# A memory-bound add in 64 KiB rows: wider loads of x and a wider middle store in the same queue

## The chip, the cores and the metric

One core of one Trainium2 chip. The metric is the device time of one execution in microseconds, lower is better. A value quoted for a kernel is the median of its runs.

## The reference, cut to what matters

```python
B, S, D = 512, 32, 640                  # x, fx: bfloat16
def reference(x, fx, alpha):            # alpha: one bfloat16
    return x + alpha * fx
```

Each of x, fx and the output holds 20.97 MB. Reading two and writing one moves 62.92 MB, and nothing can be left out.

## The kernel before

The tensors are seen as 128 partitions of 81,920 elements (160 KiB) each. A *unit* here is 16,384 elements of each partition: a row of 32 KiB on each partition, 4 MiB in all. Five units make a tensor. All large transfers are issued from SyncE (SP), and so go through one first-in-first-out queue. The add works in place in x's buffer, on VectorE (DVE).

```python
CHUNK = 16384
xs = ctx.enter_context(tc.tile_pool(name="xs", bufs=4))   # 4 x 32 KiB a partition
fs = ctx.enter_context(tc.tile_pool(name="fs", bufs=2))   # 2 x 32 KiB
...
    def compute(k, parts=1):
        n = CHUNK // parts
        for j in range(parts):
            s = bass.ts(j, n)
            nc.vector.scalar_tensor_tensor(
                out=xt[k][:, s], in0=ft[k][:, s], scalar=a_f[:],
                in1=xt[k][:, s], op0=ALU.mult, op1=ALU.add)
...
    load_x(0); load_f(0); load_x(1); load_f(1); load_x(2)      # one line each in the source
    compute(0); load_f(2); store(0); load_x(3)
    compute(1); load_f(3); store(1); load_x(4)
    compute(2); load_f(4); store(2)
    compute(3); store(3)
    compute(4, 2); store(4, 0, 2); store(4, 1, 2)              # last unit in two halves
```

In the queue this reads, with x0 for the load of unit 0 of x, f0 for that of fx, and S0 for the store of unit 0:

```
x0 f0 x1 f1 x2 f2 S0 x3 f3 S1 x4 f4 S2 S3 S4a S4b
```

Of the kernel before, what the change touches and what calls it, by code (L numbers as in the profile page):

```python
# [1 line left out]

# [4 lines left out]

ACT = mybir.ActivationFunctionType
ALU = mybir.AluOpType
F32 = mybir.dt.float32  # L10
BF16 = mybir.dt.bfloat16

CHUNK = 16384


def alpha_to_lanes(nc, consts, psum, alpha, eng):

    P = nc.NUM_PARTITIONS
    a_1 = consts.tile([1, 1], alpha.dtype, name="a_1")
    eng.dma_start(out=a_1[:], in_=alpha[None, :])  # L20
    ones = consts.tile([1, P], alpha.dtype, name="ones")
    nc.vector.memset(ones[:], 1.0)  # L22
    a_ps = psum.tile([P, 1], F32, name="a_ps")
    nc.tensor.matmul(a_ps[:], ones[:], a_1[:], start=True, stop=True)  # L24
    a_f = consts.tile([P, 1], F32, name="a_f")
    nc.vector.tensor_copy(out=a_f[:], in_=a_ps[:])  # L26
    return a_f


@with_exitstack  # L30
def kernel(
    ctx: ExitStack,
    tc: tile.TileContext,
    x: bass.AP,
    fx: bass.AP,
    alpha: bass.AP,
    out: bass.AP,
):
    nc = tc.nc
    P = nc.NUM_PARTITIONS  # L40
    xv = x.flatten_outer_dims().rearrange("(p n) d -> p (n d)", p=P)
    fxv = fx.flatten_outer_dims().rearrange("(p n) d -> p (n d)", p=P)
    ov = out.flatten_outer_dims().rearrange("(p n) d -> p (n d)", p=P)
    F = xv.shape[1]
    K = F // CHUNK
    assert K * CHUNK == F and K == 5

    consts = ctx.enter_context(tc.tile_pool(name="consts", bufs=1))
    psum = ctx.enter_context(tc.tile_pool(name="psum", bufs=1, space=bass.MemoryType.PSUM))
    xs = ctx.enter_context(tc.tile_pool(name="xs", bufs=4))  # L50
    fs = ctx.enter_context(tc.tile_pool(name="fs", bufs=2))
    ctx.enter_context(tc.manual_schedule())

    a_f = alpha_to_lanes(nc, consts, psum, alpha, nc.scalar)
    xt, ft = {}, {}

    def load_x(k):
        xt[k] = xs.tile([P, CHUNK], x.dtype, tag="x", name="x_t")
        nc.sync.dma_start(out=xt[k][:], in_=xv[:, bass.ts(k, CHUNK)])  # L59

    def load_f(k):
        ft[k] = fs.tile([P, CHUNK], fx.dtype, tag="f", name="f_t")
        nc.sync.dma_start(out=ft[k][:], in_=fxv[:, bass.ts(k, CHUNK)])

    def compute(k, parts=1):
        n = CHUNK // parts
        for j in range(parts):
            s = bass.ts(j, n)
            nc.vector.scalar_tensor_tensor(  # L69
                out=xt[k][:, s],  # L70
                in0=ft[k][:, s],
                scalar=a_f[:],
                in1=xt[k][:, s],
                op0=ALU.mult,
                op1=ALU.add,
            )

    def store(k, j=0, parts=1):
        n = CHUNK // parts
        nc.sync.dma_start(  # L80
            out=ov[:, k * CHUNK + j * n : k * CHUNK + (j + 1) * n],
            in_=xt[k][:, bass.ts(j, n)],
        )

    load_x(0)
    load_f(0)
    load_x(1)
    load_f(1)
    load_x(2)
    compute(0)  # L90
    load_f(2)
    store(0)
    load_x(3)
    compute(1)
    load_f(3)
    store(1)
    load_x(4)
    compute(2)
    load_f(4)
    store(2)  # L100
    compute(3)
    store(3)
    compute(4, 2)
    store(4, 0, 2)
    store(4, 1, 2)


# [1 line left out]
_INS = ['x', 'fx', 'alpha']  # L109
_OUTS = [((512, 32, 640), 'bfloat16')]  # L110


# [23 lines left out]
```

## Time and profile before

| | |
|---|---|
| time, median of 3 runs | 152.81 us (152.61 to 152.85) |
| span of the profiled run | 150.6 us |
| moved | 62.92 MB, 418 GB/s over the span |
| queue's share of 16 DMA engines | 98.0% |
| DVE busy | 86.9 us, 58% |

The first lines are from the page of the kernel before: busy time by engine; then the span in 40 equal slices, where a digit is the busy share in tenths and GB/s is what was moved; then the queue with its packets, megabytes and share of 16 engines.

```profile
PE 0.2 (0%) x1; PEld 0.1 (0%) x1; DVE 86.9 (58%) x8; POOL 0.2 (0%) x4
...
DMA  6999999999999999799999999999999999999994
GB/s 200 444 453 435 418 418 418 418 444 453 444 453 435 418 418 418 339 444 470 418 418 418 418 418 435 435 435 453 426 435 444 418 418 435 435 435 405 426 444 205
DMA packets 2306, 62.92 MB, mean 418 GB/s; under 512 B 258, under 2 KB 258, under 8 KB 258
...
q1 hardware_dynamic: 2304, 62.92, 98.0%
```

DMA reads 9 everywhere but at the two ends and in the slice from 60 to 64 us, where the bytes moved fall to 339 GB/s. DVE is idle for 42% of the time. So the question is how many bytes the DMA engines move per microsecond, and nothing else. The page's chain of waits and its groups look different at first sight:

```profile
DMA 56%; DVE 29%; DVEq 6%; issue 0%; SPq 0%
...
L69 DVE SCALAR_TENSOR_TENSOR x_t<-f_t,a_f,x_t 128x16384 bf16<-128x16384 bf16 (+1 forms) x6 | 86.6, 14439 | 49.5 <-DMA f_t<-in_fx_dram 49.5
...
```

The chain says that DVE's last add was released by f_t loads, and the group says that DVE waited 49.5 us for them. Both are true, and neither is a cost: while DVE waits, the queue that it waits for is full. A wait is worth something only if the thing waited for could have started earlier.

The trace also records each packet of each DMA engine. Here a packet of data is one row of one transfer: 128 rows over 16 engines, 8 for each engine, back to back. The median packet took 1213 ns for a 32 KiB row (1792 packets) and 611 ns for a 16 KiB row (256 packets). Two halves take 9 ns more than a whole. Behind its rows, each DMA sends one more packet of 4 bytes on each engine, its *completion packet*; that the DMA has *landed* is told by a semaphore event some 0.4 us later.

### The profile page before, as it was taken

How to read it: one execution, taken by the hardware profiler on the slowest of the kernel's cores; microseconds unless marked ns; L12 is line 12 of the kernel's file. 1: busy time of each engine (PE TensorE's matmuls, PEld its weight loads, DVE VectorE, ACT ScalarE, POOL GpSimd, SP SyncE). 2: the span in 40 equal slices, each digit the busy share in tenths (PEclk: the TensorE clock that was granted, in tenths of full speed). 3: DMA queues.
4: the chain of work that ended last, by engine and by line, in shares of the span. 5: the costliest groups of instructions: out<-in, count | busy, mean ns of one | idle time of the engine just before them, and what ended most of it. 6: DMA issues, size and time to landing. Idle time of an engine off the chain costs nothing.

```text
span 150.6 us, 85 instructions
## 1 busy us (share of the span) xinstructions
PE 0.2 (0%) x1; PEld 0.1 (0%) x1; DVE 86.9 (58%) x8; POOL 0.2 (0%) x4
## 2 busy tenths in 40 slices
PE   0000000000000000000000000000000000000000
PEld 0000000000000000000000000000000000000000
DVE  0000009999679998499991006999900089997000
POOL 0000000000000000000000000000000000000000
DMA  6999999999999999799999999999999999999994
GB/s 200 444 453 435 418 418 418 418 444 453 444 453 435 418 418 418 339 444 470 418 418 418 418 418 435 435 435 453 426 435 444 418 418 435 435 435 405 426 444 205
DMA packets 2306, 62.92 MB, mean 418 GB/s; under 512 B 258, under 2 KB 258, under 8 KB 258
## 3 DMA queue, kind: packets, MB, share of 16 engines
q1 hardware_dynamic: 2304, 62.92, 98.0%
q10 hardware_dynamic: 2, 0.00, 0.0%
HBM read 41.94 MB, written 20.97 MB: 418 GB/s over the span
## 4 chain that ended last, share of the span: by engine, by line
DMA 56%; DVE 29%; DVEq 6%; issue 0%; SPq 0%
DMA f_t<-in_fx_dram 56%; DVE x_t L69 29%; DVEq L131 6%; SPq L59 0%; DVEq L69 0%
## 5 line engine op out<-in xcount | busy, mean ns | idle before, releaser
L69 DVE SCALAR_TENSOR_TENSOR x_t<-f_t,a_f,x_t 128x16384 bf16<-128x16384 bf16 (+1 forms) x6 | 86.6, 14439 | 49.5 <-DMA f_t<-in_fx_dram 49.5
L26 DVE COPY a_f<-a_ps 128x1 f32<-128x1 f32 x1 | 0.2, 159 | 1.1 <-PE a_ps L24 1.1
L22 DVE MEMSET ones<- 1x128 bf16 x1 | 0.2, 165 | 0.8 <-PEq L120 0.8
L24 PE MATMUL a_ps<-a,ones 1*128 1x1 bf16 x1 | 0.2, 159 | 1.9 <-DMA a<-in_alpha_dram 1.9
L120 POOL MEMSET const-bfloat16-1.0<- 128x1 bf16 x1 | 0.1, 102 | 0.0
L120 POOL MEMSET const-uint8-127<- 128x1 uint8 x1 | 0.1, 102 | 0.0
L24 PEld LDWEIGHTS <-ones 1*128 1x128 bf16 x1 | 0.1, 100 | 1.0 <-DVE ones L22 1.0
L120 POOL MEMSET const-float32-0.0<- 128x1 f32 x1 | 0.1, 99 | 0.2 <-issue 0.2
L120 POOL MEMSET const-float32-1.0<- 128x1 f32 x1 | 0.1, 99 | 0.0
## 6 DMA issues: line engine op xcount, KB each, us to landing
x_t<-in_x_dram SPq DMA_DIRECT2D x5, 4096.0 KB, 34.8
f_t<-in_fx_dram SPq DMA_DIRECT2D x5, 4096.0 KB, 32.1
out_dram<-x_t SPq DMA_DIRECT2D x4, 4096.0 KB, 36.5
out_dram<-x_t SPq DMA_DIRECT2D x2, 2048.0 KB, 15.2
a<-in_alpha_dram ACTq DMA_DIRECT2D x1, 0.0 KB
```

What stands on the lines that cost most here:

```text
L22: nc.vector.memset(ones[:], 1.0)
L24: nc.tensor.matmul(a_ps[:], ones[:], a_1[:], start=True, stop=True)
L26: nc.vector.tensor_copy(out=a_f[:], in_=a_ps[:])
L69: nc.vector.scalar_tensor_tensor(out=xt[k][:, s], in0=ft[k][:, s], scalar=a_f[:], in1=xt[k][:, s], op0=ALU.mult, op1=ALU.add,)
L120: nc = _bacc.Bacc("TRN2", target_bir_lowering=False, num_devices=1)
L131: with _tile.TileContext(nc) as tc:
```

## The change

It moves x in pairs of units, so that a row is 64 KiB long, stores units 1 and 2 together, and keeps everything that sets the start and the end (the first unit and the last two half stores) as it was. The intent is fewer and larger packets. The order of the queue changes with it: S0 now goes ahead of f2, and loads and stores alternate less often. (U is 16384, as CHUNK was.) Two slots of 64 KiB replace the four x slots; the first one holds x0 and f0 side by side at first.

```diff
-    xs = ctx.enter_context(tc.tile_pool(name="xs", bufs=4))
+    wide = ctx.enter_context(tc.tile_pool(name="wide", bufs=1))     # tags "a" and "b", 64 KiB each
     fs = ctx.enter_context(tc.tile_pool(name="fs", bufs=2))
...
+    t_0 = wide.tile([P, 2 * U], x.dtype, tag="a", name="t_0")
+    nc.sync.dma_start(out=t_0[:, :U], in_=xv[:, :U])
+    nc.sync.dma_start(out=t_0[:, U:], in_=fxv[:, :U])
+    def load_pair(tag, u):
+        t = wide.tile([P, 2 * U], x.dtype, tag=tag, name="x_t")
+        nc.sync.dma_start(out=t[:], in_=xv[:, u * U : (u + 2) * U])
+        return t
...
+    x_12 = load_pair("b", 1)
+    f_1 = load_f(1)
+    add(t_0[:, :U], t_0[:, U:])
+    store(0, t_0[:, :U])
+    f_2 = load_f(2)
+    add(x_12[:, :U], f_1[:])
+    x_34 = load_pair("a", 3)
+    f_3 = load_f(3)
+    add(x_12[:, U:], f_2[:])
+    f_4 = load_f(4)
+    store(U, x_12[:])
+    add(x_34[:, :U], f_3[:])
+    store(3 * U, x_34[:, :U])
+    ...                                # last unit: two half adds, two half stores, as before
```

The queue now reads, with wide transfers in brackets:

```
x0 f0 [x12] f1 S0 f2 [x34] f3 f4 [S12] S3 S4a S4b
```

## The prediction

> **What bounds the kernel now.** The DMA engines. In the page's forty slices DMA reads 9 in all but the first, the last and one slice near 60-64 us; the queue table says 98.0% of 16 engines' span for q1, and 62.92 MB at 418 GB/s. DVE is busy 58% and every wait of it (49.5 us) is for an f_t landing. The chain of waits names f_t loads for 56% and DVE for 29%, but that is only the order in which things were released: the one FIFO is never empty, so a DVE wait there costs nothing.
>
> From the packet records: one packet is one row on one engine, back to back. A 32 KiB row takes 1213 ns (median of 1792), a 16 KiB row 611 ns (256). So 16 KiB cost 602 ns (27.2 B/ns, 435 GB/s over 16 engines) plus about 9 ns fixed per packet. The Trainium skill, "DMA: Bandwidth & Descriptors", Specifications, gives 435 GB/s as the fabric ceiling; this trace agrees. Nothing in the change can beat that slope.
>
> Per engine: 112 x 1.213 + 16 x 0.611 = 145.6 us. The rest of the 150.6 us span: first packet at 1.74-2.15 us, its slow first row (+0.7 us), a stall of about 0.8 us at 57.5-61 us (the last fx rows before the first store), one of 0.2 us at 87.5-90 us (before the second store), a little engine skew, and 149.4 to 150.6 us for the last receipt and end.
>
> **What the change does.** Three transfers (two x pairs, the middle store) have 64 KiB rows. Estimate: 9 + 4 x 602 = 2417 ns against 2 x 1213 = 2426, so 24 packets per engine save 9 ns each: 0.2 us. All of it is on the critical path, since the DMA is. Packets in q1 fall by 384. The same section family of the skill ("Why small descriptors are slow") puts a fixed cost on a packet; at 32 KiB it is under 1%, as measured here.
>
> Order: x0 f0 x12 f1 | S0 f2 x34 f3 f4 S12 S3 S4a S4b. Switches from load to store fall from three to two, worth perhaps 0.1 us; I expect the 0.8 us stall of the first store to move to about 50 us and stay.
>
> **Does the FIFO run dry?** With 9.7 us per unit (the trace's landings): first five units end at 51.3; S0 is issued at 40.2. f2 follows at once. x34 needs slot a, S0 landed about 62, while f2 runs to 71: 9 us margin. f3 needs the first half-pair add, 51.5+17.3 = 69, needed at 90. f4 and S12 need the second, 72+17.3 = 89, needed at 100 (11 us margin). S3: add ends 118, needed 129. Last two halves: 127 and 136, needed 139 and 144. No gap. DVE work is unchanged: 87 us (17.28 us x4, 8.75 us x2). Head (32 KiB first unit) and tail (two 2 MiB stores) are the same as before.
>
> **Predicted:** 152.81 - 0.2 - 0.1 to 0.2: 152.5 us, range 151.9 to 153.2. Faster by 2% (below 149.8) 0.01: even free packets would save only 1.1 us. Within 2% 0.95. Slower 0.04.
>
> **What would show it.** Packets of 64 KiB in the records at about 2417 ns; q1 at 1920 packets; DMA slices 9 throughout but for one dip near 50 us; DVE busy 87 us; last store landing about 149.4 us.
>
> **What would make it wrong.** A 64 KiB row being cut into pieces by the descriptor generator (gain gone, count unchanged or higher); 64 KiB stores running slower than 27 B/ns; a landing of x12 or S0 late by over 9 us, seen as a DMA slice well below 9; a longer load-to-store stall.

## The result

The changed kernel took 152.66 us (median of 6 runs, 152.32 to 152.74), the kernel before in the same rounds 152.71 us (152.51 to 152.99). The ratio is 0.9992, with a 95% interval of 0.9977 to 1.0006: the same within 2%, and not told from no change at all. A ratio here is the mean time of one kernel's runs over that of the other's of the same rounds, so it is not quite the ratio of the medians quoted. Timed once more on another chip, below, the ratio was 0.9966 (0.9944 to 0.9988).

The same lines of the page of the changed kernel:

```profile
PE 0.2 (0%) x1; PEld 0.1 (0%) x1; DVE 86.8 (58%) x8; POOL 0.2 (0%) x4
...
DMA  6999996999999899999896969999996969898994
GB/s 226 417 452 426 426 556 278 556 434 400 400 426 426 278 417 417 434 478 512 382 538 295 556 278 426 478 434 426 434 565 295 556 278 556 365 426 373 447 434 178
DMA packets 1874, 62.92 MB, mean 417 GB/s; under 512 B 210, under 2 KB 210, under 8 KB 210
...
q1 hardware_dynamic: 1872, 62.92, 97.8%
```

The queue moved the same 62.92 MB in 1872 packets in place of 2304: 384 fewer rows (three wide transfers, 128 each), and 48 fewer completion packets, as three fewer DMAs each send 16. DVE is busy as before.

The DMA line looks worse now: 6, 8 and 9 change about, and GB/s goes from 278 to 556 and back. It is an artefact of the binning. A slice is 3.8 us and a 64 KiB packet lasts 2.4 us on all 16 engines nearly in step, so whole rows fall into one slice or the next: 16 rows of 64 KiB in 3.77 us are 278 GB/s, 32 are 556, and the two average 417. Spread over the slices that each packet covers, the packet records fill every slice but the first and the last. (They do so in the stall described below, too: packets there last longer, so a busy share cannot show it.) The run of the same order in 32 KiB rows, below, shows 9s there but for one slice. A reader who took the 6s for an idle queue would look for a wait that is not there.

The chain of waits of the changed kernel:

```profile
DVE 40%; DMA 35%; another core or an unknown queue 9%; DVEq 6%; SPq 0%; issue 0%
...
```

and the piece of it that is new, from the chain in order of time (start, duration, what):

```profile
22.88 17.28 DVE t L72
40.16 12.96 another core or an unknown queue
53.12 0.03 issue
...
```

There is one core, so no other core can have released this add. It is the load f1, issued at 2.11 us and landed at 53.1 us; presumably the view does not connect a landing with an issue 51 us old. It waited for nothing but its turn in the queue.

Whether the queue ran dry is read from the issue times (start, duration, engine and line) of SP:

```profile
...
40.19 0.35 SPq L77 DMA_DIRECT2D out_dram<-t  x1
40.58 0.44 SPq L68 DMA_DIRECT2D f_t<-in_fx_dram  x1
...
62.92 0.33 SPq L63 DMA_DIRECT2D x_t<-in_x_dram  x1
70.53 19.65 SPq L68 DMA_DIRECT2D f_t<-in_fx_dram  x2
...
90.24 46.39 SPq L77 DMA_DIRECT2D out_dram<-x_t  x4
...
```

S0 was issued at 40.19 us while f1 was still to come until 53 us. f2 followed it at 40.58. The pair x34 was issued at 62.92, when f2 kept the engines busy until 72; f3 at 70.53, needed at 91; f4 and S12 at 90, needed at 101 and 111. The tightest is S4b, the last store: it was issued at 136.3, and S4a landed at 144.6. The queue always had at least 8 us of work.

So the only terms left are packets and stalls. The completion events of each DMA say when it landed. The table has the mean of its 16 events, and gives the time from one landing to the next, in us. In the kernel before, each line is one unit:

| landed | before | order_only (new order, 32 KiB rows) | after |
|---|---|---|---|
| second transfer, f0 | 9.70 | 9.71 | 9.70 |
| x1, x2 or x12 | (x1) 9.72 | 9.72, 9.71 | 19.35 |
| last load ahead of S0 | (f2) 10.42 | (f1) 10.87 | (f1) 10.94 |
| S0 | 10.08 | 9.96 | 9.98 |
| load after S0 | (x3) 9.33 | (f2) 9.45 | (f2) 9.41 |
| x3, x4 or x34 | | 9.72, 9.71 | 19.35 |
| f3 | 9.88 | 9.72 | 9.72 |
| S1, then x4 (before only) | 9.86, 9.53 | | |
| f4 | 9.72 | 9.83 | 9.72 |
| S1 and S2, S2 alone, or S12 | (S2) 9.70 | 9.71, 9.67 | 19.33 |
| S3 | 9.66 | 9.68 | 9.67 |

(Left out of before: f1 9.71 and x2 9.72.) Undisturbed, a 32 KiB unit takes 9.715 us as a load and 9.66 us as a store. A pair in 64 KiB rows takes 19.352 us as a load, which is 0.078 us under two units, and 19.332 us as a store, which is 0.05 us under the two stores of order_only in the same place. That is 2 x 0.078 + 0.05 = 0.2 us, the amount that was predicted, but it flatters the change: the two stores of order_only stand behind a load and hold some of its second stall, and against two undisturbed stores (2 x 9.66) the wide one saves nothing.

Landings have a second fault. They come 0.3 to 0.5 us behind the completion packets, 0.5 to 0.9 us for a large store with a load behind it, and in most runs the lag grows while loads follow each other (0.36 to 0.47 us in before). From the completion packets of one DMA to those of the next (mean of 16), an undisturbed DMA takes 19.320 us in 64 KiB rows, 9.681 us in 32 KiB rows, 4.862 us for 2 MiB in 16 KiB rows and 2.453 us for 1 MiB in 8 KiB rows, loads and stores alike. So a wide transfer saves 2 x 9.681 - 19.320 = 0.042 us, and the three together 0.13 us. What is not constant is the stretch around S0, and that is what the experiments ask about.

In what follows, the *switch loss* of a run is the time from the landing ahead of that stretch to the landing behind it (last load ahead of S0, S0, next load), less 2 x 9.715 + 9.66 = 29.09 us. Before: 10.42 + 10.08 + 9.33 - 29.09 = 0.75 us. After: 10.94 + 9.98 + 9.41 - 29.09 = 1.24 us. The same sum over f3, S1 and x4 of before gives 0.17 us more for its second switch, while in the changed kernel f4 and S12 stand at the undisturbed values. By completion packets the losses at S0 read up to 0.2 us higher (0.90 us before, 1.33 after), and nearly all of it is in the load ahead of S0: f2 takes 10.57 us in before and f1 11.01 us in the changed kernel, in place of 9.68, while S0 and the load behind it are undisturbed in both. The 10.08 and 9.33 in the table are one late landing.

### The profile page after: what moved, and what is told of

Read it like the earlier page. It is cut to its first block, busy times and chain, and to the rows that moved or that the text cites. A ratio compares the mean times of both kernels' runs of the same rounds, so it can differ in the third digit from the quotient of the medians. Undisturbed runs are those within 1.5% of the kernel's fastest.

```text
span 150.9 us, 78 instructions
## 1 busy us (share of the span) xinstructions
PE 0.2 (0%) x1; PEld 0.1 (0%) x1; DVE 86.8 (58%) x8; POOL 0.2 (0%) x4
## 2 busy tenths in 40 slices
DMA packets 1874, 62.92 MB, mean 417 GB/s; under 512 B 210, under 2 KB 210, under 8 KB 210
## 3 DMA queue, kind: packets, MB, share of 16 engines
q1 hardware_dynamic: 1872, 62.92, 97.8%
## 4 chain that ended last, share of the span: by engine, by line
DVE 40%; DMA 35%; another core or an unknown queue 9%; DVEq 6%; SPq 0%; issue 0%
DVE x_t L72 29%; DMA f_t<-in_fx_dram 21%; DMA t<-in_fx_dram 14%; DVE t L72 11%; DVEq L121 6%; SPq L58 0%; DVEq L72 0%
## 5 line engine op out<-in xcount | busy, mean ns | idle before, releaser
L72 DVE SCALAR_TENSOR_TENSOR x_t<-f_t,a_f,x_t 128x16384 bf16<-128x16384 bf16 (+1 forms) x5 | 69.2, 13868 | 26.9 <-DMA f_t<-in_fx_dram 26.9
L72 DVE SCALAR_TENSOR_TENSOR t<-t,a_f 128x16384 bf16<-128x16384 bf16 x1 | 17.3, 17284 | 20.6 <-DMA t<-in_fx_dram 20.6
```

The lines of the kernel that those rows point to most:

```text
L72: nc.vector.scalar_tensor_tensor(out=x_ap, in0=f_ap, scalar=a_f[:], in1=x_ap, op0=ALU.mult, op1=ALU.add)
```

## The experiments

Twelve experiments were run, four of them repeats of a kernel, each on one chip with runs of the kernel before between. All gave the right result.

### Are the 64 KiB rows or the order behind the longer stall?

order_only keeps the new order and puts every row back to 32 KiB:

```diff
-        nc.sync.dma_start(out=t[:], in_=xv[:, u * U : (u + 2) * U])
+        for j in range(2):
+            nc.sync.dma_start(out=t[:, bass.ts(j, U)], in_=xv[:, (u + j) * U : (u + j + 1) * U])
...
-    store(U, x_12[:])
+    for j in range(2):
+        store((1 + j) * U, x_12[:, bass.ts(j, U)])
```

> The new order with every row back at 32 KiB (the pair loads and the middle store as two DMAs each). Theory A (64 KiB rows save only the fixed 8 ns of 24 packets per engine, and the longer stall before the first store belongs to the order or to chance): 152.85 us, 0.2 over the changed kernel, and the stall before the first store stays at 1.2 to 1.4 us per engine. Rival B (the wide rows ahead of it lengthen that stall from 0.95 to 1.3 us): stall back at 0.95 us, time 152.5 us.

Measured: 152.53 us (152.38 to 153.20, 6 runs) against 152.45 for before, ratio 1.0012 (0.9990 to 1.0033). Its profile is of the slowest of its runs, 153.20 us. The switch loss in it is 10.87 + 9.96 + 9.45 - 29.09 = 1.18 us.

```profile
DMA  6999999999999799999999999999999999999994
GB/s 216 433 450 424 416 416 433 433 450 450 442 424 416 277 416 467 433 433 433 441 424 416 424 459 442 424 442 433 398 416 424 433 467 433 433 433 394 424 429 173
```

The 6s and 8s of the changed kernel are gone, and one dip stays, 277 GB/s in the slice from 49 to 53 us. That is the stall, which in before stood near 60 us. So a stall of this length needs no wide rows, against rival B; it is one profile, and the changed kernel itself varies from 0.94 to 1.24 us (below). The time cannot tell 152.85 from 152.5 with this spread. By completion packets order_only also lost 0.25 us in f4, ahead of its second switch; all ten profiles with wide rows in this order lost under 0.06 us there. Whether the wide rows do that is not shown by one profile.

### What does a packet cost?

rows_8k is the kernel before with each transfer cut into DMAs of 8 KiB rows, four for one (two for each half store):

```diff
+    ROW = 4096
+    def cut(dst, src, n):
+        for i in range(n // ROW):
+            s = slice(i * ROW, (i + 1) * ROW)
+            nc.sync.dma_start(out=dst(s), in_=src(s))
```

> The kernel before with all rows cut to 8 KiB, four DMAs for one. Theory A (every packet has a fixed 8 to 9 ns): 8 KiB packets of about 310 ns, 4 x 310 - 1213 = 27 ns more per 32 KiB, 120 units of 32 KiB per engine: 3.2 us slower, 156 us. Rival (the fixed part is hidden when packets follow each other, and 1213 against 611 is rounding of the records): within 0.5 us of before.

Measured: 154.25 us against 152.45, ratio 1.0113 (1.0093 to 1.0132). Slower by 1.8 us, not by 3.2.

```profile
DMA  5999999999999999999999999999999999999995
GB/s 165 425 425 434 419 417 425 423 421 421 425 421 417 428 421 421 421 432 419 436 419 419 425 425 419 436 419 423 432 417 421 423 428 421 436 423 434 419 430 213
DMA packets 8642, 62.92 MB, mean 413 GB/s; under 512 B 962, under 2 KB 962, under 8 KB 962
...
q1 hardware_dynamic: 8640, 62.92, 98.8%
```

The medians of all data packets seen, where they were not disturbed (for 8 KiB, the stores), lie on one line, 8 ns + 301 ns for each 8 KiB:

| row | 512 B | 8 KiB | 16 KiB | 24 KiB | 32 KiB | 64 KiB |
|---|---|---|---|---|---|---|
| packet, ns | 27 | 309 | 611 | 912 | 1213 | 2418 |

But these 8 ns are not all time of the queue: neighbouring records overlap by 3 to 4 ns. By completion packets (2.453, 4.862, 9.681 and 19.320 us, above) a DMA costs 0.042 us beside its bytes, which is 4.7 ns for each of the nine packets that it sends on an engine. So a packet's fixed cost is real, but the rival was half right: some 4 of the 9 ns are hidden. For the 1.8 us this gives 1.8 us of packets, and two other things, which nearly cancel. The loads ran at 2.453 us for 1 MiB at first and, from about 15 us on, at 2.485 us, another 1.05 us in all. And this run had no switch loss: by landings, 4 MiB in 8 KiB rows took 9.94 us as loads and 9.73 as stores (0.225 and 0.07 us more than in 32 KiB rows), and the three transfers around S0 took 29.65 us, against 2 x 9.94 + 9.73 = 29.61. GB/s above has no dip anywhere. Before, by completion packets, all time above the undisturbed pace was 1.13 us, so 1.8 + 1.05 - 1.13 = 1.7 us is left, near the 1.8 measured.

That was the surprise: cutting all rows to a quarter removed the stall that the change was expected to keep. Whether it was removed, or paid in small parts by the slower loads (1.05 us against 1.13), is not shown. The next runs tried to buy this for less.

### Does the first store of the program pay?

The stall of before was large at its first store (0.75 us), small at its second (0.17) and none at its third. So a first store might pay for all. early_store adds a small first store, which the last store writes over:

```diff
+    E = 256
+    z = consts.tile([P, E], x.dtype, name="z")
+    nc.gpsimd.memset(z[:], 0.0)
+    nc.scalar.dma_start(out=ov[:, F - E : F], in_=z[:])
```

> The changed kernel plus one 64 KiB store of zeros (512-byte rows, all 16 engines, from ACT's queue) at the start, to columns that the last store writes over. Theory C (the stall of about 1.3 us in the last two load rows before the first store is paid once, by the first store of the program): stall before S0 under 0.3 us, time 151.6 to 152.2 us as the cost falls into the slow first row. Rival D (each switch from loads to stores on the ring pays, or the first large store does): stall before S0 stays at 1.2 to 1.4 us, time 152.7 to 152.9 us.

Measured: 152.61 us against 152.45, ratio 1.0008 (0.9990 to 1.0026). The switch loss at S0 is 10.67 + 10.01 + 9.37 - 29.09 = 0.96 us. Theory C falls for a store from another queue. early_store_sp sends the same store from SP behind f0, so that it is in the same queue:

```diff
-    nc.scalar.dma_start(out=ov[:, F - E : F], in_=z[:])
...
+    nc.sync.dma_start(out=ov[:, F - E : F], in_=z[:])      # after the load of f0
```

> The 64 KiB store of zeros again, now from SP's own queue right behind f0, so in the same FIFO as everything else. Theory K (the first store that a FIFO meets pays the stall, whatever its size): the last rows of f0 (near 19 to 22 us) take 0.7 to 1.3 us more per engine, and the rows before S0 under 0.3 us; total unchanged, 152.7 us. Rival L (it takes a large store, or it is set by that time and order): no stall at 20 us, 0.7 to 1.3 us before S0 as in all kernels so far; 152.8 us.

Measured: 152.61 us, ratio 0.9970 (0.9947 to 0.9993), on a chip where before took 153.06 us. The switch loss at S0 is 1.08 us, and the little store landed at 22.5 us, 0.20 us after f0, with no stall beside it. Theory K falls as well: it is not simply the first store. Whether a large early store would have paid is not tried.

### The size of the rows at the switch

s0_8k cuts S0 into four DMAs of 8 KiB rows, f1_8k does this to f1, the load ahead of S0, both_8k to both, and s0_head_8k only to the first quarter of S0.

```diff
-    store(0, t_0[:, :U])                                   # s0_8k
+    for j in range(4):
+        store(j * U // 4, t_0[:, bass.ts(j, U // 4)])
...
-    f_1 = load_f(1)                                        # f1_8k (both_8k: this and the one above)
+    f_1 = load_f(1, 4)                                     # four DMAs of a quarter each
...
-    store(0, t_0[:, :U])                                   # s0_head_8k
+    Q = U // 4
+    store(0, t_0[:, :Q])
+    store(Q, t_0[:, Q:U])
```

> The changed kernel with the first store alone in 8 KiB rows (four DMAs). The run with all rows at 8 KiB had no stall before its first store. Theory F (the stall comes from the size of the store rows that follow the load: the engine reads ahead into them): stall under 0.3 us, minus 1.0, plus 8 x 27 ns = 0.2 us for packets: 0.8 us faster than the changed kernel, 151.7 us. Rival G (it comes from the size of the load rows ahead of it): stall stays at 1.0 to 1.3 us, 152.7 us.

> The changed kernel with the load just before the first store (f1) alone in 8 KiB rows, the store at 32 KiB. Theory F (size of store rows): stall stays 1.0 to 1.3 us in sum, spread over more packets, 152.8 us. Rival G (size of load rows): stall under 0.3 us, 151.7 us.

> Both f1 and the first store in 8 KiB rows. If either size or both together make the stall: stall under 0.3 us; packets cost 2 x 0.2 us; net 0.6 us faster than the changed kernel, 152.0 us. If the missing stall of the all-8-KiB run had another cause (its many DMAs elsewhere, its pace), the stall stays at 1 us and the time is 153.0 us.

> Only the first quarter of the first store has 8 KiB rows, the other three quarters have 24 KiB rows. Theory F in its read-ahead form (only the rows that are next in line when the load ends matter): stall under 0.4 us, packets 0.07 us, 151.7 to 151.9 us. If the whole store's rows matter: stall 0.8 to 1.3 us, 152.5 us.

Measured, with before at 152.64 us on this chip. From the switch loss, the cost of the 8 KiB rows themselves (0.225 for a load, 0.07 for a store) is taken off:

| run | time, us | ratio to before (95%) | switch loss, us |
|---|---|---|---|
| s0_8k | 152.71 | 1.0004 (0.9982 to 1.0026) | 1.34 - 0.07 = 1.27 |
| f1_8k | 152.22 | 0.9973 (0.9953 to 0.9992) | 0.85 - 0.22 = 0.63 |
| both_8k | 152.75 | 1.0008 (0.9989 to 1.0028) | 1.02 - 0.30 = 0.72 |
| s0_head_8k | 152.44 | 0.9988 (0.9967 to 1.0009) | 0.91 |

None reaches the 0.3 us that either theory asked for. Store rows (F) are refuted by s0_8k, load rows (G) are at best part of it, and both together leave 0.7 us. f1_8k read fastest, so it was run again beside the changed kernel.

### Repeats

f1_8k_again is f1_8k, after_timed and after_again are the changed kernel, before_again is the kernel before, all without an edit.

> The kernel that read fastest so far (f1 in 8 KiB rows, 0.9973 of before), again beside the changed kernel on one chip. If its 0.3 us less stall is real: stall 0.6 to 0.8 us, 152.2 to 152.4 us when the changed kernel has 152.6. If it was noise: within 0.1 us of the changed kernel.

> The changed kernel unaltered, five rounds beside the kernel before. By the packet sum it is 0.2 us (0.0013) faster; if the stall before its first store is on average the same as that of before: ratio 0.9987. If it is 0.2 us longer on average: ratio 1.000. Third profile of this stall: 1.0 to 1.3 us.

> The changed kernel unaltered, for how far one profile differs from the next. If the stall before the first store is a property of this order: 1.2 to 1.4 us again, and under 0.1 us before the second. If chance: anything between 0.5 and 1.5 us.

> The kernel before unaltered, for a second profile. If its stalls are a property of its order: 0.9 to 1.0 us before the first store and 0.2 to 0.3 us before the second. If chance: first 0.6 to 1.3, second 0 to 0.5 us.

| run | time, us | ratio to before (95%) | switch loss at S0, us |
|---|---|---|---|
| f1_8k_again | 152.48 | 0.9955 (0.9931 to 0.9979) | 1.24 - 0.22 = 1.02 |
| after_timed | 152.57 | 0.9966 (0.9944 to 0.9988) | 1.24 |
| after_again (one run, state unknown) | 152.41 | | 0.94 |
| before_again (one run, state unknown) | 152.69 | | 0.83, and 0.07 at S1 |

A gain of f1_8k over the changed kernel is not shown: on one chip it is 0.09 us from it, within the spread of either, and its stall came back at 1.02 us. On this third chip the kernel before was slower than elsewhere (153.06, from 152.43 to 153.54), and three kernels of the new order at 152.5 to 152.6 were not. A possible reason is in the one profile of before_again, where x1, f1 and x2 took 9.75, 9.81 and 9.87 us in place of 9.72, 0.28 us in all. But that run took 152.69 us, so it does not explain 153.06, and the difference between the chips stays open.

```profile
DMA  7999999999999998999999999999999999999994
GB/s 243 426 443 417 417 417 417 426 434 443 452 426 417 434 443 287 426 460 460 443 426 417 417 417 426 443 460 443 434 426 426 417 417 426 452 452 391 430 426 204
```

Its dip, 287 GB/s in the slice from 57 to 60 us, is where before has it, ahead of S0. So the place of the dip belongs to the order. Its size varies from profile to profile: 0.75 and 0.83 us in two profiles of before, 1.24, 0.94 and 1.24 in three of the changed kernel.

## Why the prediction was right

- **The bound.** Predicted: the DMA engines, and nothing in the change beats their slope. Shown: DVE's busy time and the queue's share hardly moved, and in every row size 8 KiB more cost 301 ns, 27.2 B/ns for each engine, 435 GB/s over 16. The Trainium skill's "DMA: Bandwidth & Descriptors", section Specifications, gives this as the fabric ceiling, and the trace agrees.
- **The packets.** Predicted: 2417 ns for a 64 KiB row and 0.2 us in all. Measured: 2418 ns, but 0.13 us in all by completion packets (at most 0.2 by landings): the prediction took a packet's 9 ns to be time of the queue, and the records overlap. The number of packets was predicted as 1920 and was 1872; the 48 completion packets of three DMAs had been forgotten. A 64 KiB row was one packet, not cut.
- **No dry queue.** The predicted margins, 8 us at the last store and 9 us and more elsewhere, held. f3 was issued at 70.5 us (69 predicted), S12 at 90 (89).
- **The switches.** Here a term of the sum failed, by 0.1 to 0.2 us: "Switches from load to store fall from three to two, worth perhaps 0.1 us; I expect the 0.8 us stall of the first store to move to about 50 us and stay". It moved to 48 to 52 us as said. But no gain from fewer switches shows. The time over the undisturbed pace at all switches was 0.75 + 0.17 = 0.92 us in the first profile of before, and 1.24, 0.94 and 1.24 us in three of the changed kernel. The kernel before also paid 0.83 + 0.07 + 0.28 (slow loads) = 1.18 us in its second profile. The sums overlap: the loss is of the same size in both orders, gathered in one place in the new one. Completion packets say the same: all time above the undisturbed pace, from the first transfer's end to the last's, is 1.13 and 1.41 us in the two profiles of before and 1.36, 1.07 and 1.38 in three of the changed kernel.
- **The total.** 0.13 us less for packets and nothing sure for switches makes 152.6 from the 152.71 of the same rounds; the measured 152.66 fits, but no change at all would fit as well. In the two first profiles the packets gave 0.13 us and the longer stalls took 0.23. The spread of single runs, 0.4 us and more, hides a gain of this size, so that the ratios of two chips (0.9992 and 0.9966) differ more than the effect.
- **"DMA slices 9 throughout".** The predicted picture was wrong for a reason of display: long packets alias with the slices.

What causes the stall is open. It sits in the last two or so rows of the load ahead of S0; it is not DVE, which is idle from 40.2 to 53.2 us in the changed kernel and so in all of the stall; it is not the program's first store as such, and not the row size of either neighbour alone or of both together, which left 0.63 to 1.27 us of it (a part may be due to the load's rows). It is absent when all transfers have 8 KiB rows. That run differs in two more ways: its loads ran at a pace some 2% lower by landings (9.94 against 9.715 us) all the way to the switch, and SP held back DMAs until earlier ones had landed:

```profile
SPq L62 <- DMA x_t<-in_x_dram: 40.8, 20, 2.2
SPq L62 <- DMA f_t<-in_fx_dram: 37.5, 18, 2.1
SPq L62 <- DMA out_dram<-x_t: 22.2, 11, 2.5
...
```

In columns: who waited, for what, us in total, times, longest. 49 short waits for landings mean that only some 1 MiB DMAs were in the queue at a time. Which of the three removes the stall was not tried.

No version timed on one chip with the changed kernel beat it beyond the noise; the others were timed only against before. By this sum, what is left to win is about 0.55 us of packets (117 on each engine, 4.7 ns each), some 1 us at the switch and 0.7 us in the first row of each engine (its packets took that much more than 1213 ns), of 152.6.

## What to carry to other kernels

Before widening rows, take two row sizes from the trace and draw the line: the fixed part times the number of packets is all that wider rows can give, here about 5 ns for each packet of over a microsecond. When DMA is at 98% with a full queue, as here, an engine's waits for loads are no cost; the new order moved the stall and did not remove it. Compare transfers by the time between their completion packets, which showed 0.04 us where the run times spread by 0.4 and where landings lag by a varying 0.3 to 0.9 us. Do not add up the lengths of packet records as if they did not overlap, and do not read the busy slices when a packet is nearly as long as a slice.

## What the Trainium skill lacked or had wrong

- "DMA: Bandwidth & Descriptors", section Measured: it gives times by transfer size, for one path, and no figure for long rows. Here 4 MiB in 8, 32 and 64 KiB rows took 9.94, 9.715 and 9.676 us as a load, by landings. Its rule of at least 1 MiB for each DMA, for 75% of peak or more, leaves a difference: 1 MiB DMAs of 8 KiB rows were 1.1% slower than 4 MiB DMAs of 32 KiB rows (size and rows changed together).
- The same page, section "Why small descriptors are slow (HBM only)": it gives a fixed overhead of about 3 cycles for each packet, and no time for it. The packet records show 8 ns at any row from 512 B to 64 KiB, of which, by completion packets, 4.7 ns are time of the queue. In 8 KiB rows, loads settled at 2.485 us for 1 MiB and stores at 2.453, which the page does not tell of.
- The same page, section "Where 436 GB/s comes from": it says that the HBM side, about 358 GB/s, binds transfers between HBM and SBUF, though it also calls a measured 425 GB/s near the fabric's rate. This core moved 418 GB/s over the whole span and 27.2 B/ns for each engine while streaming, at the fabric's ceiling. "HBM Reference", section Specifications, has it right for one core alone (about 425 GB/s).
- The same page, section "Queues, rings and completion order": an engine changes between rows of its queues at packet granularity, typically 9 to 17 descriptors to a packet. Here a turn was one row: the 64 KiB store on ACT's queue, 8 rows of 512 B on each engine, took 14.4 us from issue to landing beside SP's 32 KiB rows, and its rows started from 6.0 to 14.1 us, one about every 1.2 us on an engine. Behind SP's own f0 it took 0.2 us.
- No page that was read tells of a loss where a queue goes from loads to stores. Here, by landings, the transfers around the first large store lost 0.6 to 1.3 us, later ones 0 to 0.2 us, and with all rows at 8 KiB none lost over 0.1 us.
